# Block 5's x in another room, due steps for attention tiles, and the second MLP's first weights staged in an unused result slot

## The chip, the cores and the metric

The kernel runs on one core of a Trainium2 chip. The metric is the device time of the program in microseconds. Before the change it is 630.09 us, the median of 3 runs (629.89 to 630.75).

## What is computed

A chunked linear attention with decay feeds two MLPs, one after the other. Shapes: batch 4, 8 heads, 768 tokens, head width 32, state width 16; the attention's output is 3072 tokens by 256.

```python
# per chunk of 32 tokens, for each batch and head
cum = cumsum(log(a));  L = exp(cum_i - cum_j) * (i >= j)
y = ((C @ B.T) * L) @ x + (C @ state) * exp(cum)
state = exp(sum(log a)) * state + sum_j B_j x_j exp(cum_last - cum_j)
# first MLP: 256 -> 2048 -> 256
h = y @ w_in;  z = (h * cos(h)) @ w_out
# second MLP: 256 -> 1536 -> 256
out = (1 / (1 + exp(-(z @ w_gate))) * (z @ w_val)) @ w_out2
```

The weights come as 64-bit floats. Each matmul with weights is done in three parts: high x high, low x high and high x low, where high is the value as fp32r and low the remainder.

## The kernel before, in words

The 768 tokens are cut into six blocks of 128 tokens by 4 batches. **Attention** works through 24 tiles (block j, batch b, in the code q = 4 j + b). Blocks 0 and 1 use `add_att_chunks`, blocks 2 to 5 `add_burst`. A tile ends in `add_xt`, which splits the transposed result into `xt_hi` and `xt_lo`. There are three rooms for these x; `xt_room(j)` says which of them a block uses. A room may be written again only when the earlier block in it has gone through the first MLP.

**The first MLP** is 96 steps (block j, column group f of 16; `add_mlp1`, step number s). A step is six matmuls of 128 by 512 into a bank (`hid`), five elementwise operations on ACT, DVE and POOL that form h cos h and split it into gm, gh and gl, and six matmuls for the output (`outp`). `segs` gives the order of the steps of blocks 0 and 1: their f are cut so that block 1 starts before all weights are there. Blocks 2 to 5 follow whole, so block 5 is steps 80 to 95. A block's result lies in `x2[j]`, one of six slots.

**Weights of the first MLP** are loaded in pieces (`cuts`; `add_conv1`, `add_conv`): two loads by SP into still unused slots of x2, then four operations: `head` (L387 ACT, L389 DVE) turns the top 16 bits, `join` (L392 DVE) makes a 32-bit float, then the copy (L360) and the remainder (L365). Piece n is staged in the x2 slot that line `j = (1, 2, 4)[n] ...` names.

**The second MLP** takes two blocks at a time (18 times `add_pair`): seven products for two column groups instead of eight, with additions between PSUM banks on DVE (L1137) and copies `cp` on ACT. Its weights are 18 parts (n, p): n of six column groups, p for gate, value and output. `add_early` decodes the first six during the first MLP and stores them in DRAM (`kept`); `add_conv2` loads them back, or decodes later parts by way of `x2[0]` and `x2[1]`. Then come block sums (L526 on DVE or POOL), the copy and the remainder into `own` or into `w1`, where the first MLP's weights have been read. `open_later` gives the attention's memory to the second MLP, so nothing of `own` and `wk2` can be written before the last tile has left attention. `add_operands` forms the products' right-hand sides in the x rooms (`own_op`).

**The order.** `Order` holds all operations with the rooms they read and write. `rank` works out a key for each from the due times of the steps, backwards. `run` then places the operation that can start first by its cost model, the smaller key first where several can; the engines execute in this order, and each engine and the DMA issue of SP goes strictly in its own order. Where PE has nothing in the first microseconds, dummy matmuls (`beat`, L1264) are put in.

Of the kernel before, what the change touches and what calls it, by code (L numbers as in the profile page):

```python
# [25 lines left out]


P = dict(
    segs=((0, 0, 10), (1, 0, 9), (0, 10, 16), (1, 9, 16)),
    cuts=(0, 1, 2, 4, 6, 8, 10, 12, 14, 16),  # L30
    groups=(((0, 1), (1, 2), (2, 3), (3, 4)), ((0, 1), (1, 2), (2, 3), (3, 4))),
    raw=1,
    raw_by=('ACT', 'ACT', 'ACT', 'SP'),
    id_by='ACT',
    mask_by='ACT',
    spreads=(((1, 2), (2, 4)), ((0, 2), (2, 4)), ((0, 1), (1, 2), (2, 3), (3, 4))),
    sooner=(16000, 14500, 13000, 11500),
    t0=14000,
    stretch=(1.4, 1.0),
    hop=700,  # L40
    gap=50,
    late=150,
    warm=9000,
    fill=0.9,
    dlat=3000,
    slack=200,
    hid=-2.4,
    back=150,
    prefer=20,
    op1=1.3,  # L50
    both=6,
    early=6,
    deep=4,
)


# [9 lines left out]


class Op:
    __slots__ = ("engs", "fn", "tag", "turn", "key", "users", "left", "ready", "start", "end", "eng", "banks", "sooner", "w")


class Order:
# [17 lines left out]
        self.reads = {}  # L90
        self.sooner = 0

    def add(self, where, fn, r=(), w=(), tag=None, turn=None):
        op = Op()
        op.engs, op.fn, op.tag, op.turn, op.sooner = dict(where), fn, tag, turn, self.sooner
        op.users, op.ready, op.w = [], {e: 0.0 for e in op.engs}, w
        deps = set()
        for x in r:
            if x in self.last_w:
                deps.add(self.last_w[x])  # L100
        for x in w:
            if x in self.last_w:
                deps.add(self.last_w[x])
            deps.update(self.reads.get(x, ()))
        i = len(self.ops)
        op.banks = {x[1] if x[0] == "bank" else self.BANKS[x[0]][x[1]]
                    for x in (*r, *w) if type(x) is tuple and (x[0] == "bank" or x[0] in self.BANKS)}
        for x in r:
            self.reads.setdefault(x, []).append(i)
        for x in w:  # L110
            self.last_w[x] = i
            self.reads[x] = []
        op.left = len(deps)
        for d in deps:
            self.ops[d].users.append(i)
        self.ops.append(op)

    def rank(self):


        due, t = {}, P["t0"]
        for op in sorted((op for op in self.ops if op.turn), key=lambda op: op.turn[0]):
            t += op.engs["PE"] * P["stretch"][op.turn[1] - 1]
            due[id(op)] = t
        for op in reversed(self.ops):
            d = min((self.ops[u].key - P["hop"] for u in op.users), default=1e9)
            op.key = min(d, due.get(id(op), 1e9)) - op.sooner - min(op.engs.values()) - (P["dlat"] if "SP" in op.engs else 0)

    def run(self, beat):
# [81 lines left out]

def dve(n):

    return 64 + 1.042 * n


def dvs(n):

    return Shared(64 + 1.042 * n)


def dve2(n):

    return Shared(69 + 0.521 * n)
# [6 lines left out]
def act(n):  # L231
    return 94 + 0.833 * n
# [5 lines left out]


def pool(n):  # L240
    return 110 + 2.18 * n


@with_exitstack
def linear_attention__then__cos_mlp__then__gated_mlp_kernel(
# [68 lines left out]
    xt_lo = ring(const, 3, [128, KD, TOK], F32R, "xt_lo")  # L314

    def xt_room(j):
        return 2 if j == 2 else j % 2

    NG = 3
    gm_t = ring(const, NG, [128, TOK], F32, "gm")  # L320
# [8 lines left out]
    NL = 2  # L329
# [25 lines left out]
    def f32(t):  # L355
        return t.bitcast(F32)
# [24 lines left out]
    def add_words(n, raw, rows, top, top_r, to, to_r):  # L381

        def head(e):
            if e == "ACT":
                nc.scalar.activation(out=tops(top()), in_=heads(raw()), func=ACTF.Copy)  # L387
            else:
                nc.vector.tensor_copy(out=tops(top()), in_=heads(raw()))  # L389

        def join(e):
            nc.vector.scalar_tensor_tensor(  # L392
                out=to().bitcast(I32), in0=words(raw()), scalar=13, in1=top().bitcast(I32),
                op0=ALU.logical_shift_right, op1=ALU.bitwise_or)

        add({"ACT": act(n), "DVE": dve2(n)}, head, r=rows, w=[top_r], tag="head")
        add({"DVE": dvs(n)}, join, r=[top_r] + rows, w=to_r)

    def add_conv(fs, raw, raw_r, top, top_r, hi_lo, w_r):
# [102 lines left out]
        add_decode(n, p, j, lambda: wk1_t[i % 2][:, 0:512], ("wk1", i % 2), lambda: x2[:, j, 0:512], first)  # L502
        add({"SP": 700}, lambda e: nc.sync.dma_start(out=kept[i], in_=x2[:, j, 0:512]), r=first, w=[("kept", i)])

    def add_conv2(n, p):
        i = 3 * n + p
        wk_r = ("wk2", i % NW)
        cols = 896 if p < 2 else 512

        def wk():  # L510
            return later["wk"][i % NW]

        if i < P["early"]:
            add({"SP": 700}, lambda e: nc.sync.dma_start(out=wk()[:, 0:512], in_=kept[i]),
                r=["later", ("kept", i)], w=[wk_r])
        else:
            add_decode(
                n, p, i % 2, lambda: later["top"], "top", lambda: wk()[:, 0:512], [wk_r], ["later"])
        if p < 2:

            def block(k):
                return wk()[:, k * 128:(k + 1) * 128]

            for o, x0, x1, op in ((4, 0, 2, ALU.add), (5, 4, 1, ALU.subtract), (6, 1, 0, ALU.subtract),
                                  (7, 3, 5, ALU.subtract)):
                add({"DVE": dvs(128), "POOL": pool(128)}, lambda e, o=o, x0=x0, x1=x1, op=op: engine[e].tensor_tensor(  # L526
                    out=block(o), in0=block(x0), in1=block(x1), op=op), w=[wk_r])

        def whole():
            return wk()[:, 128:1024] if p < 2 else wk()[:, 0:512]  # L530

        hi_r, lo_r = ([(x, *y) for y in w2_room(n, p)] for x in ("hi", "lo"))
        add({"ACT": act(cols)}, lambda e: copy(e, w2_part(n, p)[:, 0], whole()), r=[wk_r], w=hi_r, tag="chi")
        add({"POOL": pool(cols), "DVE": dvs(cols)},
            lambda e: minus(e, w2_part(n, p)[:, 1], whole(), f32(w2_part(n, p)[:, 0])), r=[wk_r] + hi_r, w=lo_r, tag="clo")

# [107 lines left out]
    def add_xt(j, b):  # L644
        p = xt_room(j)
        both_ya = two_banks[pair_of(j * NB + b)][:, :, 0:128] if j < BY_HEADS else two_banks[0][:, :, 256:384]
        y_r = room_of(j * NB + b, "ya")
        o = slice(b * T, (b + 1) * T)
        xh = [("xh", p, b, k) for k in range(KD)]
        src, hi, lo = both_ya, xt_hi[p][:, :, o], xt_lo[p][:, :, o]  # L650
        if j < BY_HEADS:
            src = both_ya.rearrange("p c (k t) -> p c k t", k=KD)
            hi, lo = (x.rearrange("p k (c t) -> p c k t", c=2) for x in (hi, lo))
        add({"ACT": act(256), "DVE": dve(256)}, lambda e: copy(e, hi, src), r=y_r, w=xh, tag="xhi")
        add({"DVE": dve(256)}, lambda e: minus(e, lo, src, f32(hi)),
            r=y_r + xh, w=[("xl", p, b, k) for k in range(KD)])

    def masked(src, cm, n, by):
        return lambda e: (
# [321 lines left out]


    P6, P1, P5, P2, P3, P7, P4 = (4, 0), (0, 1), (3, 2), (2, 3), (6, 4), (5, 5), (1, 6)
    own_op = {5: ("xh", 2), 2: ("xl", 2), 0: ("xh", 0), 1: ("xl", 0), 6: ("xh", 1)}

    def operand(q):
        if q in own_op:
# [49 lines left out]
    def g_of(kind, i):  # L1037
        if i < NG:
            return {"gm": gm_t, "gh": gh_t, "gl": gl_t}[kind][i]
        return later["gm"] if kind == "gm" else xt_lo[1][:, ("gh", "gl").index(kind)]  # L1040

    def g_room(kind, i):
        if i < NG or kind == "gm":
            return [(kind, i)]
        return [("xl", 1, b, ("gh", "gl").index(kind)) for b in range(NB)]

    def add_out(n, i, when):

# [183 lines left out]
    for n in range(NP):  # L1232
        for p in range(3):
            if 3 * n + p < P["early"]:
                add_early(n, p)
    for s, step in enumerate(steps):
        j, f = step[:2]
        if 0 < j < BY_HEADS and f == 0:
            add_loads(j)
            add_atts(j)  # L1240
        if j >= BY_HEADS and f == 0:
            for q in range(j * NB - (2 if j == BY_HEADS else 0), j * NB + NB):
                add_burst(q)
        add_mlp1(s)
    att_rooms = ["a_t", "a_d"] + [
        (n, i) for n, k in (("ab", NB), ("xw", NL), ("bh", NL), ("cd", 3), ("bd", 3), ("s", NB), ("sm", 2), ("dm", 2), ("s4", NB), ("wk1", 2), ("lt", 3),
                            ("g", 3)) for i in range(k)
    ] + [(n, i, b) for n in ("xs", "an") for i in range(NL) for b in range(NB)] + [
        ("bc", i, e, b) for i in range(NL) for e in range(2) for b in range(NB)
    ] + [("stk", i, k) for i in range(3) for k in range(3)]  # L1250
    add({"NONE": 0}, open_later, w=att_rooms + ["later"])
    add({"POOL": 900, "DVE": dve2(512)}, lambda e: engine[e].memset(later["top"], 0.0), r=["later"], w=["top"])
    add_operands(0)
    for n in range(NP):
        for p in range(3):
            add_conv2(n, p)
    for n in range(NP * NJ // 2):
        if n % NP == 0 and n:
            add_operands(n // NP)
# [44 lines left out]
```

## Time and profile before

| | |
|---|---|
| runs | 630.09 us (629.89 to 630.75) |
| profiled execution | 631.17 us |
| its span, first to last instruction | 629.2 us |
| granted TensorE clock, mean | 0.995 |
| busy: PE, DVE, ACT, POOL | 612.2, 481.6, 373.8, 212.3 us |

The profile is one execution; all stretches below are microseconds from its first instruction. "PE" counts matmuls, the dummy ones too, and a matmul's end is modelled, so the count in a stretch tells more than the busy time. "PEclk" is the share of full clock that was granted. "Waits" are idle times of an engine with what ended them. L353 is the line of every matmul of the kernel, so they are told apart by their tiles: `bank<-xt_hi,w` is `hid`, `two_banks<-gh,w` is `outp`. L554 to L595 are attention's loads, L405 and L410 the first MLP's weight loads, L491 the second's.

### The profile page before, as it was taken

The page shows a single profiled execution, that of the slowest core. Times are in us where ns is not written, and L with a number is a line of the kernel's source. Part 1 is how long each engine was busy: PE and PEld are TensorE (multiplying, and loading weights), DVE is VectorE, ACT ScalarE, POOL GpSimd, SP SyncE. Part 2 cuts the span into 40 slices and gives each one's busy share as a digit, 9 for nine tenths or more (in the row PEclk, how much of TensorE's full clock was granted, in tenths as well). Part 3 has the DMA queues.
Part 4 walks back from the last instruction along what each step waited for, and adds up shares of the span by engine and source line. Part 5 has one row for each costly group of instructions (what it writes and reads, how often), then busy time and mean ns, then how long its engine had stood idle before and what let it go on. Part 6 is the DMA issues. An engine that isn't in the chain of part 4 may idle for free. (4 is left out here: it accounts for less than half of the span.)

```text
span 629.2 us, 12454 instructions
## 1 busy us (share of the span) xinstructions
PE 612.2 (97%) x4860; PEld 493.0 (78%) x4860; DVE 481.6 (77%) x812; ACT 373.8 (59%) x640; POOL 212.3 (34%) x179
## 2 busy tenths in 40 slices
PE   7989989999999999999999999999999999999996
PEld 3656768777888887887788777888888888888886
DVE  6688977699758568648888999989777778665665
ACT  1278777765766765776889664646443446444442
POOL 0023645532545444545687523414000003111000
PEclk9999989999999999999999999999999999999998
DMA  8799884366601700000221223200022000021002
GB/s 147 202 205 214 180 198 141 119 98 137 109 2 52 114 1 3 1 1 17 70 69 51 67 68 92 77 0 2 0 34 35 2 0 1 15 33 21 2 0 68
DMA packets 122826, 41.60 MB, mean 66 GB/s; under 512 B 101008, under 2 KB 120720, under 8 KB 122768
## 3 DMA queue, kind: packets, MB, share of 16 engines
q1 hardware_dynamic: 121424, 40.41, 28.5%
q8 instruction: 38, 0.62, 0.4%
q10 hardware_dynamic: 1344, 0.41, 0.3%
q14 instruction: 20, 0.16, 0.1%
HBM read 33.78 MB, written 4.92 MB: 61 GB/s over the span
## 5 line engine op out<-in xcount | busy, mean ns | idle before, releaser
L365 POOL TENSOR_TENSOR gl<-gm,gh 128x512 fp32r<-128x512 f32 x114 | 163.3, 1435 | 327.4 <-ACT gh L360 176.8
L353 PE MATMUL bank<-xt_hi,w 128*128 128x512 f32 x573 | 158.2, 395 | 5.0 <-DVE gm L944 3.9
L1137 DVE TENSOR_TENSOR bank<-bank,cp 128x512 f32<-128x512 f32 x144 | 94.6, 693 | 45.8 <-PE bank L353 41.2
L353 PEld LDWEIGHTS bank<-xt_hi,w 128*128 128x128 f32 x573 | 106.2, 189 | 28.6 <-DVE gm L944 5.2
L353 PE MATMUL two_banks<-gh,w 128*128 128x512 f32 x456 | 124.9, 393 | 0.0
L360 ACT ACTIVATE gh<-gm 128x512 fp32r<-128x512 f32 x131 | 81.8, 627 | 60.6 <-DVE gm L1165 41.0
L353 PEld LDWEIGHTS two_banks<-gh,w 128*128 128x128 f32 x456 | 85.0, 189 | 18.8 <-ACT x L974 1.0
L353 PE MATMUL bank<-xt_lo,w 128*128 128x512 f32 x318 | 94.8, 392 | 0.0
L944 DVE TENSOR_TENSOR gm<-gm,bank 128x512 f32<-128x512 f32 x96 | 65.2, 681 | 36.9 <-ACT gm L942 36.7
L938 ACT ACTIVATE gm<-bank,quarter_sb 128x512 int32<-128x512 f32 x96 | 65.7, 685 | 34.3 <-PE bank L353 21.5
L940 DVE TENSOR_TENSOR gm<-gm,bank 128x512 f32<-128x512 int32 x96 | 65.2, 682 | 17.1 <-ACT gm L938 16.6
L942 ACT ACTIVATE gm<-gm,right_sb 128x512 f32<-128x512 f32 x96 | 69.0, 720 | 13.7 <-DVE gm L940 13.2
L353 PE MATMUL two_banks<-gl,w 128*128 128x512 f32 x228 | 72.9, 395 | 0.0
L353 PEld LDWEIGHTS bank<-xt_lo,w 128*128 128x128 f32 x318 | 59.5, 189 | 12.3
L360 ACT ACTIVATE cp<-bank 128x512 f32<-128x512 f32 x72 | 43.1, 598 | 40.7 <-PE bank L353 34.6
L1162 ACT ACTIVATE gm<-bank 128x512 f32<-128x512 f32 x72 | 41.0, 598 | 38.4 <-DVE bank L1137 24.7
L353 PEld LDWEIGHTS two_banks<-gl,w 128*128 128x128 f32 x228 | 41.9, 188 | 8.8 <-issue 0.6
L1165 DVE TENSOR_TENSOR gm<-gm,bank 128x512 f32<-128x512 f32 x72 | 46.9, 680 | 2.3 <-PE bank L353 2.0
L353 PE MATMUL bank<-xt_hi,own 128*128 128x512 f32 x135 | 37.9, 392 | 0.9 <-DVE bank L1137 0.9
L353 PE MATMUL bank<-op,w 128*128 128x512 f32 x126 | 35.5, 391 | 0.0
L696 DVE TENSOR_TENSOR_SCAN lt<-ab,tt 128x512 f32<-128x512 f32 x24 | 30.2, 1262 | 0.3 <-DMA ab<-a_chunk 0.3
L353 PEld LDWEIGHTS bank<-xt_hi,own 128*128 128x128 f32 x135 | 24.9, 188 | 6.7 <-DVE bank L1137 1.7
(144 smaller groups left out, 808.7 us busy)
## 6 DMA issues: line engine op xcount, KB each, us to landing
x<-in_moe_w_out_dram SPq DMA_DIRECT2D x13, 511.5 KB
ab<-a_chunk SPq DMA_DIRECT2D x34, 128.0 KB
x<-in_moe_w_in_dram SPq DMA_DIRECT2D x7, 511.5 KB
xs<-in_x_dram SPq DMA_DIRECT2D x24, 128.0 KB
x<-in_moe_w_val_dram SPq DMA_DIRECT2D x6, 511.5 KB
x<-in_moe_w_gate_dram SPq DMA_DIRECT2D x6, 511.5 KB
out_dram<-x SPq DMA_DIRECT2D x128, 16.0 KB
bc<-in_B_dram SPq DMA_DIRECT2D x24, 64.0 KB
```

The source lines that it names most:

```text
L353: nc.tensor.matmul(out_, lhsT, rhs, start=start, stop=stop, skip_group_check=True)
L360: nc.scalar.activation(out=out_, in_=in_, func=ACTF.Copy)
L365: engine[eng].tensor_tensor(out=out_, in0=in0, in1=in1, op=ALU.subtract)
L696: add({"DVE": scan(512)}, lambda e: nc.vector.tensor_tensor_scan(out=lt, data0=ab, data1=id8.rearrange("p h t -> p (h t)"), initial=0.0, o ...
L938: add({"ACT": act_b(512) - 40}, lambda e: nc.scalar.activation(out=ri, in_=hp, func=ACTF.Identity, bias=quarter_sb), r=hr + ["round"], w=[ ...
L940: add({"DVE": dve(512)}, lambda e: nc.vector.tensor_tensor(out=g, in0=ri, in1=hp, op=ALU.subtract), r=hr, w=[("gm", u)])
L942: add({"ACT": act_b(512)}, lambda e: nc.scalar.activation(out=g, in_=g, func=ACTF.Sin, scale=-TURN, bias=right_sb), w=[("gm", u)])
L944: add({"DVE": dve(512)}, lambda e: nc.vector.tensor_tensor(out=g, in0=g, in1=hp, op=ALU.mult), r=hr, w=[("gm", u)])
L1137: add({"DVE": dve(512)}, lambda e: nc.vector.tensor_tensor(out=bank[to], in0=bank[x], in1=later["cp"][i], op=ALU.add), r=bank_r[x][:1] + [ ...
L1162: add({"ACT": act(512)}, lambda e, i=i, bk=bk: nc.scalar.activation(out=g_of("gm", i), in_=bank[bk], func=ACTF.Sigmoid), r=bank_r[bk][:1] ...
L1165: add({"DVE": dve(512)}, lambda e, i=i, bk=bk: nc.vector.tensor_tensor(out=g_of("gm", i), in0=g_of("gm", i), in1=bank[bk], op=ALU.mult), r ...
```

## The change

It puts block 5's x into room 2 instead of room 1, and block 3's alone in room 1 after block 1. The operands of the second MLP and its fourth set of gh and gl change rooms with it. It gives the last operation of each attention tile of blocks 2 to 5 a due step (`att`), which `rank` turns into a key. It prepares eight of the eighteen weight parts (`OWN`: column groups 0 and 1, and two parts of group 5) ahead of the others, decoding those not in DRAM by way of slot 5 of x2, which is empty until block 5's result; `add_later` stands in the list at block 5's second step instead of behind all steps. Four parts instead of six go by way of DRAM. The first MLP's weights come in ten pieces instead of nine and are staged in two rooms in turn from the fourth on. Blocks 0 and 1 are cut at f 8 and 12 instead of 10 and 9. Batches 2 and 3 of block 0 are loaded together, and the identity is loaded by SP's queue. Costs and margins in the planner change.

```diff
 P = dict(
-    segs=((0, 0, 10), (1, 0, 9), (0, 10, 16), (1, 9, 16)),
-    cuts=(0, 1, 2, 4, 6, 8, 10, 12, 14, 16),
-    groups=(((0, 1), (1, 2), (2, 3), (3, 4)), ((0, 1), (1, 2), (2, 3), (3, 4))),
+    segs=((0, 0, 8), (1, 0, 12), (0, 8, 16), (1, 12, 16)),
+    cuts=(0, 1, 2, 3, 4, 6, 8, 10, 12, 14, 16),
+    groups=(((0, 1), (1, 2), (2, 4)), ((0, 1), (1, 2), (2, 3), (3, 4))),
-    raw_by=('ACT', 'ACT', 'ACT', 'SP'),
-    id_by='ACT',
+    raw_by=('ACT', 'SP', 'SP', 'ACT'),
+    id_by='SP',
-    t0=14000,
+    t0=22000,
-    warm=9000,
+    warm=10000,
-    dlat=3000,
+    dlat=8000,
-    hid=-2.4,
+    hid=-1.9,
-    prefer=20,
+    prefer=120,
-    early=6,
-    deep=4,
+    early=4,
+    att=(26, 2.4),
+    deep=3,
 )
...
     def rank(self):
-        due, t = {}, P["t0"]
+        due, t, by = {}, P["t0"], []
         for op in sorted((op for op in self.ops if op.turn), key=lambda op: op.turn[0]):
             t += op.engs["PE"] * P["stretch"][op.turn[1] - 1]
             due[id(op)] = t
+            by.append((op.turn[0], t))
         for op in reversed(self.ops):
             d = min((self.ops[u].key - P["hop"] for u in op.users), default=1e9)
+            if op.due is not None:
+                d = min([d] + [t for n, t in by if n >= op.due][:1])
...
 def dve(n):
-    return 64 + 1.042 * n
+    return max(200, 64 + 1.042 * n)
...
 def pool(n):
-    return 110 + 2.18 * n
+    return 160 + 2.45 * n
...
     def xt_room(j):
-        return 2 if j == 2 else j % 2
+        return (0, 1, 2, 1, 0, 2)[j]
...
-        add({"ACT": act(n), "DVE": dve2(n)}, head, r=rows, w=[top_r], tag="head")
+        add({"ACT": 60 + 1.15 * n, "DVE": dve2(n)}, head, r=rows, w=[top_r], tag="head")
...
-    def add_conv2(n, p):
+    turns_ = [0]
+
+    def add_conv2(n, p, slot):
         i = 3 * n + p
-        wk_r = ("wk2", i % NW)
+        w_ = turns_[0] % NW
+        turns_[0] += 1
+        wk_r = ("wk2", w_)
...
             add_decode(
-                n, p, i % 2, lambda: later["top"], "top", lambda: wk()[:, 0:512], [wk_r], ["later"])
+                n, p, slot, lambda: later["top"], "top", lambda: wk()[:, 0:512], [wk_r], ["later"])
...
-        add({"DVE": dve(256)}, lambda e: minus(e, lo, src, f32(hi)),
-            r=y_r + xh, w=[("xl", p, b, k) for k in range(KD)])
+        s0, ds = P["att"]
+        add({"DVE": dve(256)}, lambda e: minus(e, lo, src, f32(hi)), r=y_r + xh, w=[("xl", p, b, k) for k in range(KD)],
+            due=s0 + ds * (j * NB + b - BY_HEADS * NB) if j > BY_HEADS else None)
...
-    own_op = {5: ("xh", 2), 2: ("xl", 2), 0: ("xh", 0), 1: ("xl", 0), 6: ("xh", 1)}
+    own_op = {5: ("xh", 1), 2: ("xl", 1), 0: ("xh", 0), 1: ("xl", 0), 6: ("xh", 2)}
...
+    def add_later():
+        att_rooms = ["a_t", "a_d"] + [
...
+        add({"NONE": 0}, open_later, w=att_rooms + ["later"])
+        add({"POOL": 900, "DVE": dve2(512)}, lambda e: engine[e].memset(later["top"], 0.0), r=["later"], w=["top"])
+        for n, p in OWN:
+            add_conv2(n, p, NJ - 1)
+
+    OWN = [(n, p) for n in (0, 1) for p in range(3)] + [(NP - 1, 0), (NP - 1, 2)]
     for s, step in enumerate(steps):
         j, f = step[:2]
+        if j == NJ - 1 and f == 1:
+            add_later()
...
-    for n in range(NP):
-        for p in range(3):
-            add_conv2(n, p)
+    for i, (n, p) in enumerate((n, p) for n in range(NP) for p in range(3) if (n, p) not in OWN):
+        add_conv2(n, p, i % 2)
```

## Rows read from the trace of the kernel before

**Rows 1.** The page, part 1: busy time of each engine.
```profile
PE 612.2 (97%) x4860; PEld 493.0 (78%) x4860; DVE 481.6 (77%) x812; ACT 373.8 (59%) x640; POOL 212.3 (34%) x179
```

**Rows 2.** Busy time by stretch; the first line names the columns.
```profile
core 0: us, PE busy (x) PEld busy (x) DVE busy (x) ACT busy (x) POOL busy (x), PEclk, DMA share, GB/s
60.00:80.00 20.00, 19.48 (x233) 13.97 (x232) 19.59 (x29) 13.93 (x21) 9.77 (x7) 1.00 0.86 187
80.00:90.00 10.00, 7.09 (x26) 5.55 (x25) 6.97 (x12) 8.69 (x14) 3.80 (x4) 0.83 0.84 160
...
120.00:140.00 20.00, 20.00 (x297) 15.74 (x295) 17.89 (x35) 12.94 (x27) 8.02 (x7) 1.00 0.49 81
200.00:280.00 80.00, 80.00 (x703) 64.98 (x702) 51.75 (x91) 56.79 (x97) 38.19 (x30) 1.00 0.18 28
300.00:340.00 40.00, 39.77 (x176) 32.39 (x175) 33.92 (x51) 33.82 (x56) 29.22 (x26) 1.00 0.21 62
340.00:400.00 60.00, 57.97 (x250) 46.34 (x249) 58.10 (x93) 38.30 (x63) 24.49 (x29) 1.00 0.27 78
450.00:500.00 50.00, 50.00 (x222) 41.41 (x221) 39.07 (x64) 19.56 (x35) 1.29 (x1) 1.00 0.14 22
```

**Rows 3.** PE's waits, 300 to 400 us: in total, times, longest.
```profile
PE bank L353 <- DVE bank L1137: 2.0, 3, 1.1
```

**Rows 4.** PE in order of time: start, us, instruction, idle before and releaser.
```profile
34.30 1.18 PE L353 MATMUL bank<-xt_hi,w 128*128 128x512 f32 x4
...
74.33 1.07 PE L353 MATMUL bank<-xt_hi,w 128*128 128x512 f32 x4
...
83.53 2.07 PE L353 MATMUL bank<-xt_hi,w 128*128 128x512 f32 x4 [2.91 <-DVE gm L944]
```

**Rows 5.** PE's waits, 0 to 100 us.
```profile
PE bank L675 <- DMA id_t<-in_ident_dram: 1.9, 1, 1.9
PE bank L675 <- DMA bc<-in_C_dram: 1.8, 2, 1.3
```

**Rows 6.** Tile xt_lo: ns min/median/max, first and last start us.
```profile
L365 DVE TENSOR_TENSOR xt_lo<-two_banks,xt_hi x24: 408/415/425, 18.3 to 297.4; 128x256 fp32r<-128x256 f32 x24
```

**Rows 7.** DVE by line, 200 to 280 us: count, busy us, mean ns.
```profile
L940 DVE TENSOR_TENSOR gm<-gm,bank 128x512 f32<-128x512 int32 x27 | 18.5, 685 | 8.5 <-ACT gm L938 8.5
L944 DVE TENSOR_TENSOR gm<-gm,bank 128x512 f32<-128x512 f32 x27 | 18.4, 683 | 16.9 <-ACT gm L942 16.9
```

**Rows 8.** DVE by line, 300 to 340 us (first row), 340 to 400 (two).
```profile
L365 DVE TENSOR_TENSOR own<-wk,own 128x896 fp32r<-128x896 f32 x4 | 5.4, 1353 | 0.2 <-ACT own L360 0.2
...
L526 DVE TENSOR_TENSOR wk<-wk 128x128 f32<-128x128 f32 x11 | 6.0, 556 | 0.1
L365 DVE TENSOR_TENSOR w<-wk,w 128x896 fp32r<-128x896 f32 (+1 forms) x5 | 5.4, 1079 | 0.0
```

**Rows 9.** Tile wk: the second MLP's block sums and joins.
```profile
L526 POOL TENSOR_TENSOR wk<-wk x27: 452/462/909, 301.4 to 407.0; 128x128 f32<-128x128 f32 x27
L526 DVE TENSOR_TENSOR wk<-wk x21: 272/430/1391, 300.0 to 392.7; 128x128 f32<-128x128 f32 x21
...
L392 DVE SCALAR_TENSOR_TENSOR wk<-x,top x12: 675/682/694, 336.9 to 409.3; 128x512 int32<-128x512 int32 x12
```

**Rows 10.** SP in order of time: when loads are issued.
```profile
23.27 0.66 SPq L405 DMA_DIRECT2D x<-in_moe_w_in_dram  x1
30.17 0.37 SPq L410 DMA_DIRECT2D x<-in_moe_w_out_dram  x1
30.58 1.13 SPq L569 DMA_DIRECT2D ab<-a_chunk  x2
```

**Rows 11.** SP's waits, 0 to 100 us.
```profile
SPq L410 <- DVE w L365: 6.0, 1, 6.0
```

**Rows 12.** All engines in order of time, 74 to 85 us.
```profile
74.84 0.42 SPq L405 DMA_DIRECT2D x<-in_moe_w_in_dram  x1
...
80.85 1.34 ACT L387 ACTIVATE wk<-x 128x1024 f16<-128x1024 bf16 x1 [2.84 <-DMA x<-in_moe_w_in_dram]
...
84.00 1.22 DVE L392 SCALAR_TENSOR_TENSOR x<-x,wk 128x1024 int32<-128x1024 int32 x1
```

More of the change, by code (lines that the diff above doesn't have):

```diff
@@ L68 @@
 class Op:
-    __slots__ = ("engs", "fn", "tag", "turn", "key", "users", "left", "ready", "start", "end", "eng", "banks", "sooner", "w")
+    __slots__ = ("engs", "fn", "tag", "turn", "key", "users", "left", "ready", "start", "end", "eng", "banks", "sooner", "w", "due")
 class Order:
@@ L91, in __init__, with add @@
         self.sooner = 0
-    def add(self, where, fn, r=(), w=(), tag=None, turn=None):
+    def add(self, where, fn, r=(), w=(), tag=None, turn=None, due=None):
         op = Op()
+        op.due = due
         op.engs, op.fn, op.tag, op.turn, op.sooner = dict(where), fn, tag, turn, self.sooner
@@ L212, in dve @@
 def dve(n):
[L214 removed]
+    return max(200, 64 + 1.042 * n)
 def dvs(n):
[L219 removed]
+    return Shared(max(200, 64 + 1.042 * n))
 def dve2(n):
@@ L503, in add_early @@
         add({"SP": 700}, lambda e: nc.sync.dma_start(out=kept[i], in_=x2[:, j, 0:512]), r=first, w=[("kept", i)])
-    def add_conv2(n, p):
+    turns_ = [0]
+    def add_conv2(n, p, slot):
         i = 3 * n + p
-        wk_r = ("wk2", i % NW)
+        w_ = turns_[0] % NW
+        turns_[0] += 1
+        wk_r = ("wk2", w_)
         cols = 896 if p < 2 else 512
         def wk():
-            return later["wk"][i % NW]
+            return later["wk"][w_]
         if i < P["early"]:
@@ L1039, in g_of @@
             return {"gm": gm_t, "gh": gh_t, "gl": gl_t}[kind][i]
-        return later["gm"] if kind == "gm" else xt_lo[1][:, ("gh", "gl").index(kind)]
+        return later["gm"] if kind == "gm" else xt_lo[2][:, ("gh", "gl").index(kind)]
     def g_room(kind, i):
@@ L1044, in g_room @@
             return [(kind, i)]
-        return [("xl", 1, b, ("gh", "gl").index(kind)) for b in range(NB)]
+        return [("xl", 2, b, ("gh", "gl").index(kind)) for b in range(NB)]
     def add_out(n, i, when):
@@ L1235, in linear_attention__then__cos_mlp__then__gated_mlp_kernel @@
                 add_early(n, p)
+    def add_later():
+        att_rooms = ["a_t", "a_d"] + [
+            (n, i) for n, k in (("ab", NB), ("xw", NL), ("bh", NL), ("cd", 3), ("bd", 3), ("s", NB), ("sm", 2), ("dm", 2), ("s4", NB), ("wk1", 2), ("lt", 3),
+                                ("g", 3)) for i in range(k)
+        ] + [(n, i, b) for n in ("xs", "an") for i in range(NL) for b in range(NB)] + [
+            ("bc", i, e, b) for i in range(NL) for e in range(2) for b in range(NB)
+        ] + [("stk", i, k) for i in range(3) for k in range(3)]
+        add({"NONE": 0}, open_later, w=att_rooms + ["later"])
[3 more added lines that the diff above has]
+    OWN = [(n, p) for n in (0, 1) for p in range(3)] + [(NP - 1, 0), (NP - 1, 2)]
     for s, step in enumerate(steps):
         j, f = step[:2]
+        if j == NJ - 1 and f == 1:
+            add_later()
         if 0 < j < BY_HEADS and f == 0:
@@ L1244, in linear_attention__then__cos_mlp__then__gated_mlp_kernel @@
         add_mlp1(s)
[L1245 to L1252, printed above, removed]
     add_operands(0)
-    for n in range(NP):
-        for p in range(3):
-            add_conv2(n, p)
+    for i, (n, p) in enumerate((n, p) for n in range(NP) for p in range(3) if (n, p) not in OWN):
+        add_conv2(n, p, i % 2)
     for n in range(NP * NJ // 2):
```

## The prediction, made before the changed kernel was run

> **What bounds the kernel now.** Read the page first: PE is busy 612.2 of 629.2 us [rows 1], so the time can only change where PE does something other than useful matmuls. A busy share does not show that, because the dummy matmuls count as busy and the ends of matmuls are modelled. So the second view is the one by stretches, and in it the number of PE instructions per stretch, not their time. In an undisturbed stretch, 450 to 500 us, 222 wide matmuls start in 50 us: one each 0.225 us [rows 2]. A step of the first MLP is twelve of them, 2.7 us. Measured by that rate, two places lose:
>
> - 300 to 400 us, where the first MLP goes over into the second: 176 + 250 = 426 matmuls where 444 would fit [rows 2], 18 short, 4.1 us. 340 to 400 holds 16 of these, and there DVE is busy 58.1 of 60 us [rows 2]. PE's waits name it: 2.0 us in three waits for DVE's additions [rows 3]; the rest of the 4.1 is in shorter holes.
> - the start. In 80 to 90 us only 26 matmuls start where 44 would fit: 18 short, 4.1 us. The granted clock there is 0.83 [rows 2]: PE stood idle 2.91 us and then began at the lower of its two levels, four matmuls in 2.07 us [rows 4] instead of 1.07. Before 80 us PE waits 1.8 us for inputs of attention (C) and 1.9 us for the identity [rows 5].
>
> After 400 us nothing is lost that the change could touch. What the change can give is therefore some 8 us, plus what the start can be shortened by.
>
> **The change part by part.**
>
> *Rooms and due steps.* Block 5's x now goes into room 2, free after block 2 (step 47), not room 1, free after block 3 (step 63). A tile of attention of blocks 2 to 5 gets a due step 26 + 2.4 n, n counted from block 2's first tile; the last is due at step 62, not 80. Before, the last tile is written at 297.4 us [rows 6], just ahead of block 5. No instruction is added. PE's work is the same, so the price is only in whether DVE can follow: sixteen tiles in 36 steps. A step costs DVE 0.685 + 0.683 = 1.37 us [rows 7]. In 200 to 280 us there are 27 steps and 4 tiles' worth: (51.75 - 27 x 1.37) / 4 = 3.7 us of DVE a tile, and (80 - 27 x 2.7) / 4 = 1.8 us of PE [rows 2, 7]. Over the 36 steps: DVE 49.3 + 59.2 = 108.5 of 97.2 + 28.8 = 126 us, 86%. At 120 to 140 us DVE runs at 17.89 of 20 and PE shows no idle time [rows 2]. So I cost it at nothing (ends: 0, and +2 if a tenth of the tile work stood before PE).
>
> *Staging in the unused slot.* With attention over by step 62 the second MLP's rooms open some 18 steps, 48 us, before block 5 begins, where DVE has 48.6 - 18 x 1.37 = 24 us free. Eight of the eighteen weight parts are now prepared there, the decoded ones by way of x2's slot 5. Their DVE work at most: four joins of 0.68, ten block sums at the median 0.43 (of twenty; POOL takes half, as it took 27 of 48 before), eight remainders of 1.08, which is 2.7 + 4.3 + 8.6 = 15.6 us [rows 8, 9]. It fits. Before, twelve joins run from 336.9 to 409.3 us [rows 9], one each 6.6 us, behind six parts prepared first. After, ten are left, and they can begin when block 5 leaves its first weights, near 305; at the same pace they end near 305 + 60 = 365, half under the first MLP. In 340 to 400 the sums and remainders alone take 6.0 + 5.4 us of DVE and nine joins 6.2 [rows 8, 9]; with more than half of it gone DVE falls below 50 of 60 us, and the additions that PE waits for are no longer queued. I take -3.0 of the 4.1 us (ends: 0 and -4.1); what stays is the switch itself. Behind it nothing is late: block 5's result must wait for slot 5 to be read, which is over 40 us earlier. Two parts fewer go by way of DRAM; SP is idle then, nothing.
>
> *A rule that speaks against this.* Under the first MLP POOL is busy 38.19 of 80 us, 1.27 us an instruction [rows 2], and DVE's remainders for the weights took 1.35 us there against 1.08 later [rows 8]. The Trainium skill, page "SBUF — State Buffer", section "Who interferes with whom", says that a DVE instruction with two SBUF inputs and a GpSimd instruction reading SBUF exclude each other for the whole instruction. By the row the moved work grows by 8 x 0.27 = 2.2 us and still fits in 24, and the sum stays; by the rule at its hardest it does not fit, and the time is that of the second rival.
>
> *The start: queue of SP.* SP issues in order. At 23.27 it issues a weight load of the first MLP (f 4 and 5) and then stands until 30.17, 6.0 us of it for a staging room that DVE has not left [rows 10, 11]; behind it are block 1's loads, from 30.58 on. The new cuts and rooms put f 3 and f 4 into rooms that come free later still, so their loads stand behind block 1's in the order. Then these go out up to 6 us earlier, and PE's 1.8 us for C goes: -1.8 (ends: 0 if SP stands before another room, and -1.8).
>
> *The start: identity from ACT's queue to SP's, merged loads of batches 2 and 3, raw_by.* The 1.9 us [rows 5] lies where dummy matmuls fill PE until the first step. That step needs tiles 2 and 3 and weights, so an earlier identity is hidden: 0 (ends: +0.5, one more issue ahead of the others, and -1.9).
>
> *The start: segments 8 and 12.* Before, block 1's x is there when its first step starts, 74.33 [rows 4], after ten steps, with DVE busy 19.59 of 20 us in 60 to 80 [rows 2]. After, it is due after eight steps: two steps (2.7 us of DVE) and the decoding of f 8 and 9 (join and remainder, 1.22 us [rows 12] and about as much again) leave the chain ahead of it. So block 1 starts about 5 us earlier, two steps (5.4 us) poorer: 0. What it does change is the next 30 us: f 8 on is first needed at step 16. Before, ACT stood in order before the decode of a load issued at 74.84 until 80.85 [rows 12], and the sines behind it cost PE the 4.1 us. With 8 steps of room such a decode need not stand there, but the order is planned and the loads' landing is only estimated; I take half, -2.0 (ends: 0 and -4.1).
>
> *The start: fewer staging rooms.* Three pieces ahead instead of four: f 3's load waits for f 2's decode (done soon after the second step's start at 34.30 [rows 4], say 36) where it was out before 23.27 [rows 10]. A load takes some 6 us [rows 12], its decode four operations near 0.7 (half a piece of 1.22): f 3 is ready at 43 to 45. From 34.3 to 69 PE has seven steps and four tiles, 18.9 + 7.2 of 34.7 us, 8.6 us of slack. I take +0.6 (ends: 0 and +5).
>
> *Planner numbers* (costs of POOL, DVE and ACT, slack, margins): they only reorder; 0, within the ends above.
>
> Sum: -3.0 - 1.8 - 2.0 + 0.6 = -6.2. The profiled execution took 631.17 us (span 629.2, 1.97 around it), 1.08 above the median 630.09. 631.17 - 6.2 - 1.08 = 623.9 us.
>
> **The rivals.**
>
> 1. *Slower: weights starve PE at 36 to 60 us.* With two staging rooms in turn, f 3 comes 5 us late and f 6 and 7 again 5 us, and each hole lets the clock fall as the one before 83.53 did (+1.0 on the next four matmuls [rows 4]). That is 2 x (5 + 1) = 12 us, of which the 8.6 us of slack take up some or none. For it: SP's 6.0 us wait shows that the rooms are short [rows 11]; against it: the work ahead of block 1 shrinks. It decides when block 1's first step starts no earlier than before, after 74.3, with two steps less done. With half of the slack used: 623.9 + 12 - 4.3 = 631.6; ends 627 and 636.
> 2. *The weights stay late.* If gl on POOL and the weights' operations on DVE shut each other out, eight remainders and twenty sums that wait 1.27 us each need 36 us more where 24 are free; the parts pile up as before and the transition keeps its loss. That also covers the due steps not moving the tiles. 623.9 + 3.0 = 626.9.
> 3. *The start gains all that it can:* the hole at 80 goes whole (-2.1 more), the identity brings 1.9, staging costs nothing (-0.6): 619.3.
> 4. *No net change:* the transition stays and the hole at 80 comes back elsewhere: 623.9 + 3.0 + 2.0 = 628.9, 0.2% under the median before.
>
> **How the numbers follow.** Forecast 0.44; slower 0.14; weights late 0.17; full start 0.17; no net change 0.08. Above 630.5 lies most of the slower case, 0.09; below 617 there is 0.06, for a start that moves as a whole; so the range is 617.0 to 630.5. A difference under 0.2% (1.3 us) can't be told from none. Faster: 0.44 + 0.17 + 0.17 = 0.78; same 0.08; slower 0.14.
>
> **What would show it.** The last xt_lo of attention near 250 us instead of 297.4; the first write of own near 255 to 270; the last join before 375; 340 to 400 us with over 260 matmuls and DVE below 52 us; no standing of SP before block 1's loads; 40 or more matmuls in each 10 us from 74 on; block 1's first step near 69. The forecast is wrong if 340 to 400 keeps its 250 matmuls, or if block 1 starts after 74 us.

## The result and the profile after

| kernel | median us | ratio to before, 95% interval |
|---|---|---|
| the change | 624.95 (623.54 to 626.65, 6 runs) | 0.9917 (0.9892 to 0.9942) |
| before, beside it | 629.99 (629.2 to 632.5, 6 runs) | |
| the change again (after2) | 625.55 | 0.992 (0.9899 to 0.9941) |

The forecast was 623.9 in 617.0 to 630.5. One kernel's runs spread over several us (before: 624.58 to 631.56 in 32 runs), so small parts are read from the traces, and the times only settle what is larger than some 1.5 us.

Page of the changed kernel, part 1, to set beside [rows 1]:

```profile
PE 608.6 (97%) x4845; PEld 492.9 (79%) x4845; DVE 476.7 (76%) x820; ACT 374.3 (60%) x643; POOL 200.0 (32%) x172
```

The span is 624.4 us, 4.8 less. PE's share is still 97%: as before, the share does not show where the time went. The stretches of [rows 2], changed kernel (columns as there):

```profile
60.00:80.00 20.00, 19.94 (x221) 15.21 (x218) 17.72 (x29) 15.95 (x24) 9.78 (x7) 1.00 0.90 188
80.00:90.00 10.00, 9.25 (x40) 6.99 (x39) 7.84 (x12) 7.99 (x12) 4.76 (x4) 1.00 0.83 197
120.00:140.00 20.00, 20.00 (x267) 16.10 (x266) 15.16 (x31) 13.59 (x25) 9.43 (x8) 1.00 0.74 121
200.00:280.00 80.00, 80.00 (x917) 64.19 (x916) 60.06 (x110) 57.95 (x102) 37.21 (x36) 1.00 0.23 46
300.00:340.00 40.00, 40.00 (x178) 32.96 (x177) 30.95 (x48) 35.26 (x59) 25.04 (x22) 1.00 0.18 53
340.00:400.00 60.00, 59.33 (x261) 48.51 (x260) 53.78 (x89) 38.50 (x63) 19.53 (x19) 1.00 0.15 44
450.00:500.00 50.00, 50.00 (x222) 41.42 (x221) 37.64 (x62) 20.37 (x35) 1.29 (x1) 1.00 0.14 22
```

The undisturbed rate is the same (222 in 50 us). In 300 to 400 us 178 + 261 = 439 matmuls start instead of 426: 13 x 0.225 = 2.9 us (taken as one stretch the two numbers are 437 and 424, since a matmul that crosses the bound at 340 counts on both sides). In 80 to 90 us there are 40 instead of 26, at full clock. In 200 to 280 us DVE carries 60.06 instead of 51.75 us and PE shows no idle time: the due steps cost nothing. PE's only wait left in 300 to 400 us, where [rows 3] had 2.0 us for DVE's additions:

```profile
PE bank L358 <- ACT gm L1172: 0.7, 1, 0.7
```

Tiles of the changed kernel, against [rows 6] and [rows 9]: the last xt_lo of attention at 254.8 us instead of 297.4, and the parts of `own` and the joins from 266.0 and 279.7 on:

```profile
L370 DVE TENSOR_TENSOR xt_lo<-two_banks,xt_hi x24: 414/420/428, 16.6 to 254.8; 128x256 fp32r<-128x256 f32 x24
...
L365 ACT ACTIVATE own<-wk x8: 617/939/961, 266.0 to 311.0; 128x896 fp32r<-128x896 f32 x5, 128x512 fp32r<-128x512 f32 x3
...
L397 DVE SCALAR_TENSOR_TENSOR wk<-x,top x14: 679/685/1806, 279.7 to 387.7; 128x512 int32<-128x512 int32 x14
```

The start, in PE instructions that read the first MLP's weights (the view by stretches, only tile w; the PE count is the first number in brackets, PEclk stands after the five engines). Eight tiles of attention have been done by 100 us in every kernel here, so the counts up to there can be compared. Before:

```profile
30.00:60.00 30.00, 19.73 (x74) 13.36 (x75) 4.40 (x5) 4.23 (x5) 0.00 (x0) 1.00 0.88 203
60.00:100.00 40.00, 32.94 (x131) 24.97 (x130) 4.85 (x4) 3.68 (x4) 0.00 (x0) 0.96 0.77 175
0.00:100.00 100.00, 52.66 (x204) 38.34 (x205) 9.81 (x9) 8.54 (x9) 0.00 (x0) 0.98 0.82 185
```

After:

```profile
30.00:60.00 30.00, 18.71 (x58) 12.80 (x58) 4.99 (x6) 3.38 (x4) 0.00 (x0) 0.83 0.90 207
60.00:100.00 40.00, 36.36 (x154) 28.47 (x155) 4.96 (x5) 4.21 (x4) 0.00 (x0) 1.00 0.79 179
0.00:100.00 100.00, 55.80 (x214) 41.57 (x215) 9.95 (x10) 8.85 (x10) 0.00 (x0) 0.95 0.83 184
```

It is 16 poorer in 30 to 60 us, at a granted clock of 0.83, and 23 richer in the next 40. With the two that start before 30 us it is 10 ahead over the whole 100 us (214 against 204), 2.2 us. With the 2.9 of the transition that makes 5.1 us, a little more than the 4.8 by which the span is shorter. In its second profile (after2) the changed kernel has 218 by 100 us, 14 ahead, 3.2 us.

PE in order of time, changed kernel, against [rows 4]:

```profile
31.53 0.95 PE L358 MATMUL bank<-xt_hi,w 128*128 128x512 f32 x2 [2.10 <-DVE w L370]
...
33.20 2.06 PE L358 MATMUL bank<-xt_hi,w 128*128 128x512 f32 x4
...
43.52 2.06 PE L358 MATMUL bank<-xt_hi,w 128*128 128x512 f32 x4
...
68.54 1.07 PE L358 MATMUL bank<-xt_hi,w 128*128 128x512 f32 x4
```

The step of f 3 starts at 43.52 (forecast 43 to 45), block 1's first step at 68.54 (forecast near 69; before 74.33). Twice four matmuls take 2.06 us instead of 1.07: the lower clock, once after PE stood 2.10 us for f 0's remainder, once after the waits at 40 to 43 us. SP's loads, against [rows 10]: block 1's are out at 23.97 instead of 30.58.

```profile
23.40 0.47 SPq L415 DMA_DIRECT2D x<-in_moe_w_out_dram  x1
23.97 1.13 SPq L578 DMA_DIRECT2D ab<-a_chunk  x2
```

But PE's waits in 0 to 100 us, against [rows 5], have not gone; they have other owners:

```profile
PE bank L358 <- DVE w L370: 2.1, 1, 2.1
PE bank L685 <- DMA id_t<-in_ident_dram: 1.3, 1, 1.3
PE two_banks L358 <- DMA xs<-in_x_dram: 0.9, 1, 0.9
PE two_banks L358 <- DVE cd L699: 0.9, 1, 0.9
PE bank L358 <- ACT w L365: 0.8, 1, 0.8
PE bank L685 <- DMA bc<-in_C_dram: 0.8, 1, 0.8
```

### The profile page after: what moved, and what is told of

It is laid out like the page before. It is cut to its first block, busy times and chain, and to the rows that moved or that the text cites. A ratio compares the mean times of both kernels' runs of the same rounds, so it can differ in the third digit from the quotient of the medians.

```text
span 624.4 us, 12429 instructions
## 1 busy us (share of the span) xinstructions
PE 608.6 (97%) x4845; PEld 492.9 (79%) x4845; DVE 476.7 (76%) x820; ACT 374.3 (60%) x643; POOL 200.0 (32%) x172
## 4 chain that ended last, share of the span: by engine, by line
PE 87%; DMA 4%; SPq 3%; DVE 3%; ACT 1%; issue 1%; DVEq 0%; ACTq 0%
PE bank L358 46%; PE two_banks L358 39%; DMA x<-in_moe_w_out_dram 2%; SPq L563 1%; DMA xs<-in_x_dram 1%; PE bank L887 1%; SPq L569 1%; DVE w L370 1%; DVE gm L954 1%; DMA a_chunk<-ad 1%; SPq L578 0%; DVE bank L1147 0%; DVE gm L950 0%; SPq L410 0%; SPq L415 0%
## 5 line engine op out<-in xcount | busy, mean ns | idle before, releaser
L370 POOL TENSOR_TENSOR gl<-gm,gh 128x512 fp32r<-128x512 f32 x110 | 157.2, 1431 | 276.2 <-ACT gh L365 133.1
L365 ACT ACTIVATE gh<-gm 128x512 fp32r<-128x512 f32 x135 | 84.1, 627 | 55.3 <-DVE gm L1175 32.9
```

The costliest lines, as they stand in the source:

```text
L365: nc.scalar.activation(out=out_, in_=in_, func=ACTF.Copy)
L370: engine[eng].tensor_tensor(out=out_, in0=in0, in1=in1, op=ALU.subtract)
```

## The experiments

Ten kernels beside the changed one, one of them twice. The kernel before, timed beside them, had medians of 629.42 us (b_rooms, b_start, a_nodue, a_ownlate), 628.22 (a_oldrooms, a_segs, o_f3slot0, b_latehead) and 630.34 (the other three and after2), so kernels are compared by the ratio and not by the medians. "In 300 to 400" is the number of PE instructions there (before 424, changed 437, 444 at the undisturbed rate), each from one profile. Some waits move behind 400 us, so the last column has 300 to 450 too (before 644, changed 658, 666 at the undisturbed rate).

| kernel | median us | ratio, 95% interval | in 300 to 400 | in 300 to 450 |
|---|---|---|---|---|
| b_rooms: before + rooms, due steps, staging | 625.0 | 0.9935 (0.9912 to 0.9959) | 438 | 658 |
| b_start: before + start and planner numbers | 625.8 | 0.9963 (0.9941 to 0.9986) | 432 | 650 |
| a_nodue: change without due steps | 625.33 | 0.9942 (0.9922 to 0.9963) | 436 | 654 |
| a_ownlate: change without slot 5 | 623.28 | 0.9916 (0.9889 to 0.9942) | 442 | 662 |
| a_oldrooms: change with the old rooms | 626.46 | 0.997 (0.9955 to 0.9986) | 431 | 649 |
| a_segs: change with the old segments | 625.48 | 0.9954 (0.9935 to 0.9974) | 436 | 657 |
| o_f3slot0: a_ownlate + third staging room | 622.56 | 0.9902 (0.9876 to 0.9927) | 442 | 663 |
| the same again (o_f3slot0b) | 623.38 | 0.9894 (0.9872 to 0.9915) | 442 | 663 |
| b_latehead: before, one decode later | 629.31 | 1.0013 (0.9995 to 1.0032) | 425 | 644 |
| b_lateheads: before, seven decodes later | 628.51 | 0.9968 (0.9952 to 0.9985) | 424 | 643 |
| b_roomslate: before + rooms, due steps | 626.6 | 0.9951 (0.9931 to 0.9971) | 434 | 653 |

**The two halves.** b_rooms has the second half of the change and all else of before (the edit in part):

```diff
     def xt_room(j):
-        return 2 if j == 2 else j % 2
+        return (0, 1, 2, 1, 0, 2)[j]
...
-    early=6,
+    early=4,
+    att=(26, 2.4),
...
```

> The kernel before with the rooms, the due steps, four kept parts and the early staging in slot 5 alone; segments, cuts, staging rooms of the first MLP's weights, queues and planner costs are those of before. Theory (the transition is paid for by the second half of the change, the start by the first): the last xt_lo near 255 us, 340 to 400 us with 260 or more PE instructions instead of 250, the start up to 100 us as before, some 627 us (630.0 - 2.9). Rival (the planner's new numbers clear the transition, or the rooms alone only move work about): 250 to 253 instructions in 340 to 400 us and 629 to 631 us.

b_start is the reverse: the new `P` (but early=6) and cost functions, old rooms, no due steps, no add_later.

> The kernel before with the new segments, cuts, groups, staging rooms, queues and planner numbers, but the old rooms, no due steps, six kept parts and no early staging. Theory: 340 to 400 us keeps its 250 PE instructions, the gain of the start stays (2 us and a little more by 100 us), some 627.8 us. Rival (start and transition hang together, the start's gain is lost by other collisions later): within 1 us of 630.

b_rooms in 300 to 400 us:

```profile
300.00:400.00 100.00, 99.50 (x438) 81.73 (x437) 83.29 (x131) 72.04 (x117) 48.16 (x45) 1.00 0.16 48
```

b_start:

```profile
300.00:400.00 100.00, 98.94 (x432) 80.12 (x430) 87.95 (x138) 73.80 (x119) 49.50 (x46) 1.00 0.23 69
```

The theory holds for b_rooms in the transition: the second half alone regains 14 matmuls, 3.2 us, as much as the whole change does. It is wrong on the transition of b_start: there attention still ends at 291.6 us and nothing is staged early, and yet 8 matmuls, 1.8 us, come back (6 up to 450 us), although the time is what the theory named (0.9963 of 630 is 627.7). The first half of the change alone clears about half of the transition; whether its planner numbers or its start do it was not separated. The halves do not add there; in the times (0.65% and 0.37%, together 0.83% for the change) this can't be told.

They do not visibly add at the start either. b_rooms has the start of before and yet 217 matmuls by 100 us, as many as the two profiles of the changed kernel (214 and 218); b_roomslate, with that start too, has 218, and b_latehead and b_lateheads, in which decodes were moved, 205 and 223. The interval of b_rooms overlaps that of the change. So it is not shown that the new start saves time on top of the new rooms. Tile w, b_rooms and then after2:

```profile
0.00:100.00 100.00, 54.57 (x217) 39.55 (x218) 9.80 (x9) 8.54 (x9) 0.00 (x0) 1.00 0.81 187
...
0.00:100.00 100.00, 55.24 (x218) 41.35 (x219) 9.96 (x10) 8.84 (x10) 0.00 (x0) 0.93 0.83 184
```

**Within the second half.** Three kernels undo one part each of the changed kernel.

```diff
-            due=s0 + ds * (j * NB + b - BY_HEADS * NB) if j > BY_HEADS else None)
+            due=None)
```

> The changed kernel without due steps; rooms and early staging stay. Theory (the due steps are what brings attention forward, since the planner otherwise puts the tiles behind by their keys): the last xt_lo goes back towards 290 us, the second MLP's parts are written to own from 295 us on, the loss in 340 to 400 us comes back to 250 to 254 instructions, some 627.5 us. Rival (the room alone lets the tiles go early): last xt_lo before 270 us and the time of the changed kernel, 625.

The tiles go back, as expected (last xt_lo at 291.1, first write of own 299.7), but most of the loss does not come back: 436 matmuls in 300 to 400.

```profile
300.00:400.00 100.00, 99.17 (x436) 81.27 (x435) 91.74 (x137) 76.06 (x125) 51.98 (x53) 1.00 0.23 74
```

DVE is as busy there as before the change (91.74 against 92.02 of 100 us), and PE loses little; up to 450 us it keeps 10 of the 14 matmuls gained. So neither early attention nor a lighter DVE is needed for most of the gain.

```diff
     def xt_room(j):
-        return (0, 1, 2, 1, 0, 2)[j]
+        return 2 if j == 2 else j % 2
```

(with `own_op` and the fourth gh and gl turned back alike)

> The changed kernel with the old rooms (block 5's x in room 1, free only after block 3); due steps and early staging stay. Theory (due steps can't be met when the room isn't free): block 5's tiles come after step 63, the last xt_lo at 270 us or later instead of 254.8, and 340 to 400 us loses about half of what was gained, 255 instructions; some 626 us. Rival (the due steps do all of it): last xt_lo before 260 us and the time of the changed kernel, 625.

The tiles still end at 256.4 us, so the due steps alone bring them forward and the rival was right on that. The time went the theory's way, 431 matmuls:

```profile
300.00:400.00 100.00, 99.25 (x431) 79.95 (x430) 89.89 (x138) 71.11 (x115) 45.43 (x39) 1.00 0.17 53
```

What the rooms give, 6 matmuls (9 up to 450 us, 2.0 us), they do not give by moving the tiles. By what is open: DVE's 89.89 us here is less than the 91.74 of a_nodue, which starts five matmuls more. Of the kernels that undo one part this is the only one whose interval (0.9955 to 0.9986) lies clear of that of the change, which is 0.53%, 3.3 us, faster.

```diff
-        for n, p in OWN:
-            add_conv2(n, p, NJ - 1)
...
-        if j == NJ - 1 and f == 1:
-            add_later()
...
+    add_later()
     add_operands(0)
-    for i, (n, p) in enumerate((n, p) for n in range(NP) for p in range(3) if (n, p) not in OWN):
-        add_conv2(n, p, i % 2)
+    for n in range(NP):
+        for p in range(3):
+            add_conv2(n, p, (3 * n + p) % 2)
```

> The changed kernel with rooms and due steps, but all eighteen parts prepared in their old order behind the steps and staged in x2's slots 0 and 1 (four by way of DRAM); slot 5 is not used. Theory (early staging itself takes the work out of the jam): parts that need slots 0 and 1 begin only after their operands are formed near 290 to 300 us; 340 to 400 us loses half of what was gained, 255 instructions, some 626.3 us. Rival (early memory is enough, the staging slot brings nothing): 625.0 us, 260 instructions.

The rival, and more than it: without slot 5 nothing is lost at all.

```profile
300.00:400.00 100.00, 100.00 (x442) 82.53 (x441) 87.64 (x146) 71.77 (x117) 42.79 (x40) 1.00 0.22 69
```

Its joins run to 403.9 us, 16 us longer than in the changed kernel, without one wait of PE between 300 and 450. Staging in slot 5 does not bring the gain. That it costs something is not shown either, for with the start and the planner costs of before it is the other way round:

> The start and the planner costs of before, the new rooms and due steps, and the parts prepared in the old order without slot 5. Theory (rooms and due steps alone clear the transition): a loss of under 1.2 us in 300 to 450 us, 263 or more PE instructions in 340 to 400, 2 to 3 us from the new start missing: 624.8 us. Rival (the old order of the parts needs the new planner costs): 252 to 258 instructions and 627 us.

(b_rooms with the same edit.) 434 matmuls, four fewer than b_rooms, and 626.6 us: the rival's time, though 340 to 400 us has 262, next to what the theory named, and the loss lies in 300 to 340. To leave out slot 5 gives 5 matmuls or costs 4, as the rest of the plan stands; in the times neither is clear of the spread.

```profile
300.00:400.00 100.00, 98.93 (x434) 80.73 (x433) 88.42 (x138) 73.83 (x122) 47.12 (x47) 1.00 0.23 69
```

**What stood before the additions.** How busy DVE is does not decide how many matmuls start, so here are the three waits of [rows 3], followed back on DVE. The longest, in the kernel before:

```profile
383.94 2.12 POOL L365 TENSOR_TENSOR w<-wk,w 128x896 fp32r<-128x896 f32 x1 [1.50 <-ACT w L360]
384.04 2.30 DVE L362 CAST gh<-gm 128x512 fp32r<-128x512 f32 x1
386.26 1.28 DVE L1137 TENSOR_TENSOR bank<-bank,cp 128x512 f32<-128x512 f32 x2
...
387.60 0.96 PE L353 MATMUL bank<-xt_hi,w 128*128 128x512 f32 x3 [1.14 <-DVE bank L1137]
```

A copy to gh, in the median of DVE's 19 copies 0.43 us long, took 2.30 us here, until POOL had finished a weights' remainder; the addition came behind it. The other two waits look the same: at 356.30 a gh of 1.12 us beside POOL's remainder from 352.62 to 354.76, at 364.31 a gl of 1.59 us instead of 0.68 beside the one from 360.93 to 362.50. From one matmul's start to the next these three holes cost 2.5 us beyond the undisturbed 0.225. PE waits for DVE's additions seventeen times in 300 to 450 us, in before, the two kernels with later decodes, b_start, a_nodue, a_oldrooms and b_roomslate. Each time such a held DVE operation, 1.1 to 2.3 us long, stands in the four us before, and in all but one DVE works without a gap from there to the addition. Not every overlap holds DVE (a gh at 360.94 took 0.42 us though POOL's remainder had begun at 360.93), and not every hold makes PE wait: in the changed kernel a gh is held too (1.36 us, at 381.01), and no wait of PE follows. No run moves POOL's work by itself, so that this is the cause is read from the traces and not shown by an edit.

**The hole at 80 us.** What ACT waited for in the kernel before, 60 to 110 us:

```profile
ACT wk L387 <- DMA x<-in_moe_w_in_dram: 3.1, 2, 2.8
```

b_latehead keeps this decode from standing there:

```diff
-        add({"ACT": act(n), "DVE": dve2(n)}, head, r=rows, w=[top_r], tag="head")
+        add({"ACT": act(n), "DVE": dve2(n)}, head, r=rows + list(late), w=[top_r], tag="head")
...
-    for n, f in enumerate(cuts[:-1]):
+    for n, f in enumerate(cuts[:-2]):
...
+        if s == 13:
+            add_conv1(len(cuts) - 2, cuts[-2], cuts[-1], [("gh", s % NG)])
```

> The kernel before, in which the decode of the last weight piece (f 14 and 15) waits for step 13's gh, so that ACT can't stand before it at 80 us. Theory (the hole at 80 us is ACT standing in order before a load): 80 to 90 us with 40 or more PE instructions instead of 26, no wait of ACT for a weight load there, some 626 us. Rival (the hole only moves, another operation stands there instead): 629 to 630 us.

The hole only moved, as the rival said: 29 instructions in 80 to 90 us, and ACT now stands before the decode of another load.

```profile
ACT wk L387 <- DMA x<-in_moe_w_gate_dram: 2.7, 1, 2.7
```

b_lateheads does the same to the six early parts, at steps 18 to 28.

> The kernel before, in which the decodes of the last weight piece and of all six early parts of the second MLP wait for gh of later steps (13 and 18 to 28), so that no decode of a load can be placed on ACT around 80 us. Theory (in b_latehead another decode, of w_gate, took the place before which ACT stands): no wait of ACT for a weight load in 74 to 90 us, 80 to 90 us with 40 or more PE instructions instead of 26 and 29, some 626 us. Rival (PE lacks work there for another reason, block 1's first steps wait for their own chain through ACT and DVE): below 34 instructions and 628 to 630 us.

```profile
80.00:90.00 10.00, 9.53 (x39) 6.77 (x38) 6.31 (x14) 7.06 (x13) 6.40 (x6) 1.00 0.88 187
```

No wait of ACT for a load is left in 70 to 92 us, PE has 39 instructions, and the kernel is 0.32% (0.15 to 0.48) faster, 2.0 us; the transition has its 424 as before. So ACT standing in order before a load is the hole, as the theory said, but it is worth about 2 us in the mean, half of what the one profile showed, and the time (628.51) is the one that the rival named. A likely reason for the half, from one pair of profiles: in b_rooms, with the same instructions in the same order between 66 and 83 us, that load was waited for 1.5 us instead of 2.84, PE stood 1.59 us and the clock did not fall.

**The start.** a_segs has the old segments in the changed kernel.

> The changed kernel with the old segments of blocks 0 and 1 (ten and nine columns groups instead of eight and twelve). Theory (eight steps ahead of block 1 cost nothing and take the hurry from the late weights): the eighth xt_lo 3 to 6 us later than in the changed kernel (68.1), a hole of 2 to 4 us between 70 and 100 us, some 626.5 us. Rival (the segments are neutral): within 0.7 us of the changed kernel.

The eighth xt_lo comes at 77.1 us instead of 68.1, and 60 to 100 us has 137 matmuls on w where the change has 154:

```profile
60.00:100.00 40.00, 33.85 (x137) 26.12 (x136) 4.87 (x4) 4.19 (x4) 0.00 (x0) 0.96 0.73 170
```

30 to 60 us has 11 more than the change (69 against 58); over the first 100 us it has 205 where the two profiles of the change have 214 and 218, so it is 9 to 13 behind, 2 to 3 us. By the time it is 0.37% behind the change, in intervals that overlap: the theory's side, not settled. The hole of 2 to 4 us in 70 to 100 that the theory named is not there.

o_f3slot0 gives f 3's piece a room of its own in a_ownlate:

```diff
-        j = (1, 2, 4)[n] if n < 3 else 2 * (n % 3) if n < P["deep"] else 2 + 2 * (n % 2)
+        j = (1, 2, 4, 0)[n] if n < 4 else 2 * (n % 3) if n < P["deep"] else 2 + 2 * (n % 2)
```

> The kernel with new rooms and due steps whose parts are prepared in the old order (a_ownlate), and f 3's piece staged in x2's slot 0, a third room, so that its load need not wait for f 2's decode. Theory (the rooms cost the start some us between 35 and 45): f 3's load out before 25 us, its step some 3 to 5 us earlier, 10 more wide matmuls by 60 us, 621.5 to 622.5 us. Rival (block 1's x decides, the slack hides the late weights): no difference to a_ownlate beyond 0.7 us, 623.3.

The edit did not do what it was meant to: behind f 2's no weight load goes out before 30.72 us (29.02 in a_ownlate), since SP's order has block 1's first loads ahead of it. So the step of f 3 starts no earlier (42.98 in a_ownlate, 44.52 here), block 1's first step is at 67.12 and 69.00, and what an earlier load would be worth stays open.

```profile
44.52 2.08 PE L358 MATMUL bank<-xt_hi,w 128*128 128x512 f32 x4
```

The time is not worse for it. Beside the changed kernel:

> The changed kernel again, beside the others on one chip. Between the shares of the parts found so far (rooms and due steps some 3.5 us, start some 2): 624 to 625 us. If the parts do not add: 626 us or more.

> The new rooms and due steps, the parts in the old order and f 3's piece in slot 0, beside the changed kernel on one chip. Theory (slot 5 costs the transition 1.2 us, the third staging room brings the start about 1): 2 us under the changed kernel, 622.5 us. Rival (both are noise of the start): within 0.7 us of the changed kernel.

625.55 and 623.38 us; the ratios 0.992 and 0.9894 have intervals that overlap. The version without slot 5 and with the third room beats the kernel before by 1.0% twice. By the ratios it is 0.9 and 1.6 us ahead of the changed kernel (2.2 by the medians above), which the intervals do not tell from nothing. Its transition accounts for five matmuls, 1.1 us of it.

## Why the prediction was right, point by point

The time came out 1 us above the forecast, well inside the range. The sum is right in its largest term (for another reason than the one given), right in the hole at 80 us, and wrong in SP's queue.

- *Transition, -3.0 of 4.1.* Measured 13 matmuls, 2.9 us; with b_rooms alone 3.2. The size was right. 340 to 400 us has 261 instructions (forecast over 260); DVE is at 53.78 us, not below 52, and the last join at 387.7, not before 375. The step behind the size failed: "with more than half of it gone DVE falls below 50 of 60 us, and the additions that PE waits for are no longer queued". a_nodue gains 12 of 13 (10 of 14 up to 450 us) with DVE as busy as ever, a_ownlate gains most with joins until 403.9 us, b_start gains 8 of 13 (6 of 14) with attention where it was. So that the size was right is in part luck. What the traces show in place of the amount of work is its place: each of PE's waits for an addition stands behind a DVE operation held to 1.1 to 2.3 us while POOL ran. How the plan comes to avoid that in each kernel is not settled.
- *Due steps, 0.* Right: the tiles end at 254.8 us (forecast near 250), DVE does 60 of 80 us where 200 to 280 us holds more of them, and PE has no gap there. The room, which was to make it possible, is not what moves the tiles: with the old rooms they end at 256.4 us.
- *The hole at 80 us, -2.0 (half).* Right in mechanism: 40 instructions in the changed kernel, 14 more than before, 3.2 us of this one profile; the two edits of the kernel before show that it is ACT's order, and 2.0 us in the mean when it is taken away. That the new segments are what takes it away is not shown: b_rooms, with the old ones, has 37.
- *Segments, 0, block 1 near 69 us.* Block 1 started at 68.54; a_segs puts the worth at 2 to 3 us by its one profile, 0.37% by the times, not clear of zero.
- *Fewer staging rooms, +0.6.* The step of f 3 came at 43.52, in the stretch forecast, but by luck: its weights were done at 39.7 us (its remainder is below), and PE stood in order before attention's C, cd and x instead. Block 1 was not late for it. What a third room would give was not tested, as its load went out no earlier. The slower rival, which was built on this, fell by the same rows.

```profile
39.01 0.67 DVE L370 TENSOR_TENSOR w<-x,w 128x512 fp32r<-128x512 f32 x1
```

- *SP's queue, -1.8.* This is the term that failed. Block 1's first loads went out 6.6 us earlier, as forecast, but the wait for C did not go with them. It fell from 1.8 to 0.8 us in this profile and is 2.4 us in the second (below); it is 1.1 to 2.8 us in the five profiles with the old start and 0.6 to 3.5 in the nine with the new one. PE comes to the later C sooner too (39.64 us instead of 44.48) and waits there again. In the first profile 2.1 and 0.8 us of waiting for f 0's weights, 0.9 for x and 0.9 for cd stand beside it, and the clock fell twice. The start gave 2.2 us there and 3.2 in the second profile, where 1.8 + 2.0 - 0.6 = 3.2 were forecast, but the 14 matmuls of 80 to 90 us alone are 3.2. The miss in the time, 1.05 us between 623.9 and 624.95, lies within the spread of the runs.

```profile
PE bank L685 <- DMA bc<-in_C_dram: 2.4, 2, 2.2
```

- *The rival of late weights.* The Trainium skill, page "SBUF — State Buffer", section "Who interferes with whom", lets a DVE instruction with two SBUF inputs and a GpSimd instruction that reads SBUF shut each other out. The trace agrees: in the changed kernel DVE's block sums took 279 / 286 / 1403 ns (shortest, median, longest), and the longest, at 260.59, ran beside a gl of POOL of 1.29 us from 260.55. The median shows that it is rare, and the eight parts were done by 321 us, so the rival fell. But the forecast took such holds for a price on the work that was moved; in the kernel before they stood in the transition itself, ahead of the additions that PE waits for.

```profile
L535 DVE TENSOR_TENSOR wk<-wk x25: 279/286/1403, 260.6 to 390.2; 128x128 f32<-128x128 f32 x25
```

## What to carry to other kernels

Count the instructions of the bounding engine per stretch against its undisturbed rate: it gave the size of both losses before the change was run, though not their mechanism. For the mechanism, look for operations on the engine waited for that took longer than their like, and not only at how busy it is. Where an order is planned, undo each part by itself before crediting it: here each half alone, and the change without due steps, without its rooms or without its staging slot, regained 7 to 18 of the 20 lost matmuls. An operation that an in-order engine holds for a load costs what is queued behind it; here moving one such operation let the next take its place, and only moving all seven removed the hole.

## What the runs showed of the hardware that was not expected

A DVE operation was held to several times its usual length while POOL ran, also one with a single input: the copy to gh took 2.30 us beside a POOL remainder of 2.12 us where the median of its kind is 0.43.

One kernel's start differs between executions by as much as the parts studied here: PE waited for C 0.8 us in one profile of the changed kernel and 2.4 us in the other, for f 0's remainder 2.1 and 0.7. Between before and b_rooms, with the same order up to there, the same load at 80 us was waited for 2.84 and 1.5 us, and only the longer wait was followed by the lower clock (0.89 against 1.00 in 80 to 84 us, 0.68 against 1.00 in 84 to 88). A single profile of the start is therefore good to 2 us at best, while 300 to 400 us repeats to a matmul (437 and 437, 442 and 442 in the two kernels that were profiled twice).
